# Two attention and feed-forward layers on one core: the second chunk's second weights and its last second products in another place of the order

## The chip, the core and the metric

The kernel runs on one core of a Trainium2 chip. Such a core has engines with instruction streams of their own: TensorE (PE) multiplies matrices, VectorE (DVE), ScalarE (ACT) and GpSimd (POOL) work on elements, SyncE (SP) mostly issues transfers. Each engine runs its own list strictly in order and waits on semaphores for the others. The metric is the device time of the whole program in microseconds (us).

## The reference, cut to what matters

One sequence of 2048 tokens with 576 numbers each goes twice through an attention layer and a feed-forward layer, with the same weights both times, all in fp32:

```
x = x + attention(layernorm(x), wqkv, wo)
x = x + silu(layernorm(x) @ w1) @ w2
x = x + attention(layernorm(x), wqkv, wo)
x = x + silu(layernorm(x) @ w1) @ w2
```

`w1` is 576 x 4608 and `w2` is 4608 x 576. The attention is sliding and dilated: 32 heads of 18 numbers, and token t sees only the tokens t, t-2, ..., t-14 (those that exist). Its logits and weighted sums are small products per token; the large matrix products are those of `wqkv`, `wo`, `w1` and `w2`.

## The kernel before, in words

**Chunks.** The tokens are cut into four chunks of 512 (four tiles of 128 tokens). With two layers that makes eight steps, numbered s = 0 to 7 in the code: attention, projection and feed-forward of the first, second, third, fourth chunk, and then the same again for the second layer. The front of a step (its attention on VectorE, the projection with `wo`, line L853, and the preparation of the feed-forward input) runs beside the feed-forward of the step before it. Where this document says "the second chunk" and "the third chunk" it means s = 1 and s = 2, in the first layer.

**Products.** Numbers that go through TensorE are split into a high and a low half in fp16; three matmuls (high by high, high by low, low by high) give one fp32 product.

**Two kinds of feed-forward.** Steps 0 and 1 use `ffn`. There the 4608 hidden numbers are 36 tiles of 128, taken in groups (of 9 for the second chunk, four groups). For each tile of a group there is a *first product* of 14 matmuls of 512 columns (L1192), written to one of two PSUM banks (z), then silu and scaling on ScalarE (L1194, L1196) and the low half on VectorE (L1199), which gives h. Then, for each of the four token tiles j, the *second products* (L1211) sum the nine h of the group into an accumulator (acc, two of them): three thirds of 18 matmuls of 288 columns. VectorE adds the accumulator to x (L860). Step 2 on use `ffn_pairs`: the first product is made in 2 x 2 blocks by a scheme with seven *block products* instead of eight (P5, P1, P3, P6, P2, P7, P4 in the order of `P_ORDER`), each 7 matmuls of 256 columns (L1095), with weights prepared once in DRAM (wfs). ScalarE copies some of the sums out (L1099), VectorE adds others (L1102), then come silu (L1118, L1120, L1122) and the two halves of h (L1125, L1128); second products (L1150) stand between the next block products.

**Forms.** Block products need seven sums and differences of the blocks of the layer-normalised input, called forms here. Each is made from two parts: ScalarE copies a high half (L1060, L1061) into a buffer yh or yo, VectorE subtracts for the low half (L1064, L1065), and SyncE transposes the part by a DMA (L1070) into the area xb. There are two buffers, used in turn, and each holds both parts of one form.

**Loads.** SyncE issues the weight loads: first weights of a tile (w1s, L865, 320 KB), second weights of a tile (w2s, L870, 288 KB), block weights (wfs, L1025, 160 KB each), and also the transposes of the projection's input (L465). GpSimd issues other transfers. First weights have 6 slots and block weights 12 in the same memory; second weights have 11 slots for all steps.

**What sets the order.** The code does not emit instructions at once. Each piece of work is an `op` with an engine, an estimated duration, what it reads and writes, and a priority (smaller goes first). A planner, `Plan.order`, simulates the engines, slots and transfers with these estimates, and on each engine takes the ready piece of the smallest priority whose slots are free. The instructions are then written in that order. In step s the products have priority pp = s + 0.5, and loads, ScalarE and VectorE work pd = s - 0.5. The block products of pair q have pp + 0.01 q, and their second products pp + 0.01 (...) + 0.005. The argument `after` adds an operation that the planner must have finished first; it moves an instruction in the lists, and no wait on the chip comes from it. `ffn_pairs` already uses it: `after=begun[-2:-1]` holds second weights of a pair back until an earlier pair has begun.

The functions that the diff touches, and what calls them:

Of the kernel before, what the change touches and what calls it, by code (L numbers as in the profile page):

```python
# [26 lines left out]
NJ = 4  # L27
# [5 lines left out]
NFT = F // P  # L33
# [231 lines left out]
def sliding_attention_silu_ffn(ctx: ExitStack, tc: tile.TileContext, x, wqkv, wo, w1, w2, out):  # L265
# [6 lines left out]
    op = S.op  # L272

    def fl(t):
        return t.rearrange("p a b -> p (a b)")
# [5 lines left out]
    def T(b):  # L281
        return S.tags[b.tag][b.slot]
# [154 lines left out]
    def passes(xk, wk):  # L437

        for k in range(4):
            yield xk(k), wk(k)  # L440
            yield xk(k), wk(5 + k)
            yield xk(5 + k), wk(k)
        yield xk(4), wk(4)
        yield xk(4), wk(9)
# [25 lines left out]
    PACE_WQ, PACE_WO, PACE_W = (1, 7, 0, 6), (2, 2, 3, 3, 3), (4, 5, 6, 7)  # L470
    gate = []
    formed = []
    begun = []
    highs = []
    turned = []
# [387 lines left out]
    def load_w1(f, prio):  # L863
        w = Buf("w1")
        op("SP", 0.38, lambda: nc.sync.dma_start(fl(T(w)), w1s[f]), [("w1s", f)], [w], prio, nbytes=P * 20 * P)  # L865
        return w

    def load_w2(f, prio, kind="w2", after=()):
        w = Buf(kind)
        op("SP", 0.38, lambda: nc.sync.dma_start(fl(T(w)), w2s[f]), [("w2s", f)], [w], prio, nbytes=P * 4 * D, after=after)  # L870
        return w
# [293 lines left out]
    def ffn(s, xT, xs):  # L1165
        raw = s == 0
        n, i = (G0, 0) if raw else (G1, 1)
        pp, pd = s + 0.5, s - 0.5
        for g in range(NFT // n):
            hb, wbs = [], []  # L1170
            if raw:
                ws = []
                for f in range(g * n, (g + 1) * n, NB):
                    for q in range(0 if f == 0 else NB, 2 * NB):
                        raw_load(f + q, -0.98 if f < NB else pd)
                    ws += raw_split(f, -0.98 if f < NB else pd)
                group_scale(0, g, g * n, (g + 1) * n)
            for f in range(g * n, (g + 1) * n):
                if raw:
                    wa, wb = ws[f - g * n]  # L1180
                    ka, kb = [(wa, 0), (wa, 1)], [(wb, 0), (wb, 1)]
                else:
                    wa, wb = load_w1(f, pd), load_w2(f, pd)
                    ka, kb = [wa], [wb]
                z, hs, h = Buf("z"), Buf("hs"), Buf("h")
                hb.append(h)
                wbs.append((wb, kb))

                def mm(z=z, wa=wa):
                    pl = list(passes(lambda k: T(xT)[:, k, :], lambda k: T(wa)[:, k, :]))  # L1190
                    for m, (u, v) in enumerate(pl):
                        nc.tensor.matmul(T(z), v, u, start=m == 0, stop=m == len(pl) - 1)  # L1192
                op("PE", 3.02, mm, [(xT, j) for j in range(NJ)] + ka, [z], pp)
                op("ACT", 0.61, lambda z=z, hs=hs, f=f: nc.scalar.activation(T(hs), T(z), AF.Silu, scale=d1[:, f:f + 1]),  # L1194
                   [z, ("s12", f)], [hs], pd, table="silu")
                op("ACT", 0.65, lambda hs=hs, h=h, f=f: nc.scalar.activation(T(h)[:, 0, :], T(hs), AF.Copy,  # L1196
                                                                             scale=shs[i][:, f:f + 1]),
                   [hs, ("sh", i, g)], [(h, 0)], pd)
                op("DVE", 0.68, lambda hs=hs, h=h, f=f: nc.vector.scalar_tensor_tensor(  # L1199
                    T(h)[:, 1, :], T(hs), shs[i][:, f:f + 1], T(h)[:, 0, :], op0=ALU.mult, op1=ALU.subtract),  # L1200
                   [hs, (h, 0), ("sh", i, g)], [(h, 1)], pd)
            for j in range(NJ):
                acc = Buf("acc")
                step = n if n < 6 else 3

                for t in range(0, n, step):
                    def mm2(j=j, acc=acc, t=t, step=step, hb=hb, wbs=wbs):
                        for q in range(t, t + step):
                            for m, (a, w) in enumerate(((0, 0), (0, 1), (1, 0))):
                                for h in range(2):  # L1210
                                    nc.tensor.matmul(T(acc)[:, h, 0:288], T(hb[q])[:, a, j * P:(j + 1) * P],  # L1211
                                                     T(wbs[q][0])[:, w, h * 288:(h + 1) * 288],
                                                     start=q == 0 and m == 0, stop=q == n - 1 and m == 2)
                    op("PE", 0.737 * step, mm2, [(hb[q], a) for q in range(t, t + step) for a in range(2)]
                       + [k for q in range(t, t + step) for k in wbs[q][1]], [acc], pp)
                op("DVE", 0.75, lambda j=j, acc=acc, g=g: add_to(xs[j], acc, d2s[i][:, g:g + 1]),
                   [acc, ("sh", i, g)], [xs[j]], pd)
        if raw:
            tables()
            pair_scale()  # L1220
        write_x(s, xs)
# [114 lines left out]
```

## Time and profile before

| | us |
|---|---|
| median of 3 runs | 2147.14 (2143.12 to 2147.98) |
| the profiled execution | 2146.88 |
| its span | 2144.9 |
| TensorE busy | 2115.3 (99% of the span) |
| VectorE busy | 1641.4 (77%) |
| ScalarE busy | 975.7 (45%) |
| GpSimd busy | 363.8 (17%) |

The granted TensorE clock is 0.999 of full speed over the whole execution. The second chunk's feed-forward ends at 684.66 us, and the third chunk's block products begin there.

How to read rows: in a group, `L1150 PE MATMUL acc<-w,h ... x5184 | 668.2, 286 | 1.5 <-DVE x L860 0.9` is line 1150 on TensorE, output and inputs by the program's names, the count, the busy time in us and the mean of one in ns, and behind the second bar the idle time of the engine just before these instructions with what ended most of it. In a timeline a row has its start and length in us, and the idle time before it in brackets. A row of transfers gives the queue, the count, the size of each and the median time from issue to landing in us. In a table of windows each engine has its busy time with the number of instructions in parentheses; then come the granted clock, the share of the DMA engines and GB/s.

### The profile page before, as it was taken

The page shows a single profiled execution, that of the slowest core. Times are in us where ns is not written, and L with a number is a line of the kernel's source. Part 1 is how long each engine was busy: PE and PEld are TensorE (multiplying, and loading weights), DVE is VectorE, ACT ScalarE, POOL GpSimd, SP SyncE. Part 2 cuts the span into 40 slices and gives each one's busy share as a digit, 9 for nine tenths or more (in the row PEclk, how much of TensorE's full clock was granted, in tenths as well). Part 3 has the DMA queues.
Part 4 walks back from the last instruction along what each step waited for, and adds up shares of the span by engine and source line. Part 5 has one row for each costly group of instructions (what it writes and reads, how often), then busy time and mean ns, then how long its engine had stood idle before and what let it go on. Part 6 is the DMA issues. An engine that isn't in the chain of part 4 may idle for free.

```text
span 2144.9 us, 41358 instructions
## 1 busy us (share of the span) xinstructions
PE 2115.3 (99%) x16233; PEld 1576.3 (73%) x16233; DVE 1641.4 (77%) x2599; ACT 975.7 (45%) x1803; POOL 363.8 (17%) x585
## 2 busy tenths in 40 slices
PE   9999999999999999999999999999999999999999
PEld 5556566656666788877788777887788877888887
DVE  8999999999877998558975499755997569853322
ACT  7555788644344554334433343343443434333332
POOL 2224656233232240001100010000000000000000
PEclk9999999999999999999999999999999999999999
DMA  6576777687888988676758755586555965566551
GB/s 182 158 224 249 251 267 249 189 280 238 191 210 256 298 255 248 153 224 169 220 133 194 218 173 174 139 246 182 168 166 147 254 180 161 163 156 198 155 168 62
DMA packets 334235, 426.21 MB, mean 199 GB/s; under 512 B 145608, under 2 KB 262708, under 8 KB 330072
## 3 DMA queue, kind: packets, MB, share of 16 engines
q1 hardware_dynamic: 293720, 293.19, 49.4%
q0 software_dynamic: 38304, 129.28, 19.2%
q8 instruction: 127, 2.08, 0.4%
q10 hardware_dynamic: 2016, 1.11, 0.2%
q14 instruction: 68, 0.56, 0.1%
HBM read 307.32 MB, written 67.68 MB: 175 GB/s over the span
## 4 chain that ended last, share of the span: by engine, by line
PE 76%; DVE 10%; DMA 8%; issue 5%; POOL 1%; ACT 1%; SPq 0%; DVEq 0%; ACTq 0%; POOLq 0%
PE acc L1150 26%; PE z L1095 12%; PE misc L1095 11%; PE z L681 8%; PE misc L681 5%; PE z L1192 5%; PE acc L853 4%; PE acc L1211 4%; DMA w<-wfs 2%; DMA wq<-in_B_w_dram 2%; DVE xa L1015 1%; DVE prs L814 1%; DMA xb<-yh 1%; DVE prs L821 1%; DVE prs L781 1%
## 5 line engine op out<-in xcount | busy, mean ns | idle before, releaser
L1150 PE MATMUL acc<-w,h 128*128 128x288 f16 x5184 | 668.2, 286 | 1.5 <-DVE x L860 0.9
L1150 PEld LDWEIGHTS <-h 128*128 128x128 f16 x5184 | 507.2, 98 | 126.5 <-issue 1.9
L1095 PEld LDWEIGHTS <-w 128*128 128x128 f16 x5292 | 517.1, 98 | 76.3 <-DMA w<-wfs 7.3
L1095 PE MATMUL z<-xb,w 128*128 128x256 f16 x2674 | 338.7, 273 | 6.0 <-DMA w<-wfs 4.7
L1095 PE MATMUL misc<-xb,w 128*128 128x256 f16 x2618 | 330.8, 273 | 1.5 <-ACT yo L1099 0.9
L860 DVE SCALAR_TENSOR_TENSOR x<-acc,d,x 128x576 f32<-128x576 f32 x183 | 148.4, 813 | 133.1 <-PE acc L1150 124.0
L1211 PE MATMUL acc<-w,h 128*128 128x288 f16 x1728 | 214.3, 286 | 0.0
L681 PEld LDWEIGHTS <-xa 128*128 128x128 f16 x1344 | 131.0, 98 | 113.3 <-issue 2.5
L1211 PEld LDWEIGHTS <-h 128*128 128x128 f16 x1728 | 168.4, 98 | 44.5
L814 DVE TENSOR_TENSOR prs<-kvs,pe 128x1152 f32<-128x1152 f32 x128 | 170.7, 1352 | 0.7
L781 DVE TENSOR_TENSOR prs<-qt,kvs 128x2304 f32<-128x2304 f32 x64 | 163.4, 2553 | 10.0 <-DMA kvs<-kvs 9.1
L785 DVE TENSOR_REDUCE lg<-prs 128x128 f32<-128x2304 f32 x64 | 163.1, 2548 | 1.0
L821 DVE TENSOR_TENSOR prs<-prs 128x1152 f32<-128x1152 f32 (+1 forms) x128 | 135.2, 1056 | 3.2
L1192 PE MATMUL z<-xb,w 128*128 128x512 f16 x588 | 130.5, 382 | 5.3 <-ACT hs L1194 1.8
L1128 DVE SCALAR_TENSOR_TENSOR h<-wq,sh,h 128x1024 f16<-128x1024 f32 x60 | 76.9, 1281 | 70.6 <-ACT h L1125 70.5
L681 PE MATMUL z<-wq,xa 128*128 128x432 f16 x630 | 120.4, 346 | 0.4 <-ACT w L694 0.4
L853 PE MATMUL acc<-wo,yo 128*128 128x288 f16 x896 | 114.4, 286 | 3.7 <-DMA yo<-yh 1.7
L1099 ACT ACTIVATE wq<-z 128x256 f32<-128x256 f32 x95 | 36.1, 380 | 174.3 <-PE z L1095 174.2
L1192 PEld LDWEIGHTS <-w 128*128 128x128 f16 x588 | 57.7, 99 | 75.5 <-issue 4.0
L681 PE MATMUL misc<-wq,xa 128*128 128x432 f16 x546 | 105.5, 346 | 2.6 <-ACT xa L463 1.3
L853 PEld LDWEIGHTS <-yo 128*128 128x128 f16 x896 | 87.3, 98 | 27.9 <-DMA yo<-yh 4.0
L762 POOL DMA_DIRECT2D kvs<-kvs x64 | 33.8, 535 | 419.7 <-ACT qt L750 419.7
(229 smaller groups left out, 2575.2 us busy)
## 6 DMA issues: line engine op xcount, KB each, us to landing
w<-wfs SPq DMA_DIRECT2D x756, 160.0 KB, 3.3
w<-w2s SPq DMA_DIRECT2D x252, 288.0 KB, 4.0
wq<-wqs SPq DMA_DIRECT2D x17, 1080.0 KB, 6.5
kvs<-kd POOLq DMA_DIRECT2D x8, 1584.0 KB, 9.7
w<-w1s SPq DMA_DIRECT2D x36, 320.0 KB, 5.8
wfs<-xa POOLq DMA_DIRECT2D x18, 640.0 KB, 5.4
w2s<-w POOLq DMA_DIRECT2D x36, 288.0 KB, 4.2
w1s<-wq POOLq DMA_DIRECT2D x30, 320.0 KB, 3.4
```

Of the source, the lines that this page charges most:

```text
L681: nc.tensor.matmul(T(m)[:, :3 * UC], a, b, start=n == 0, stop=n == len(pl) - 1)
L781: nc.vector.tensor_tensor(T(pr), T(qt)[:, j:j + 2, None, :].to_broadcast([P, 2, W, UC]), win(T(kv), j, 2), op=ALU.mult)
L785: nc.vector.tensor_reduce(T(lg)[:, j:j + 2].rearrange("p a w h -> p (a w h)"), T(pr).rearrange("p a w (h d) -> p (a w h) d", d=DH), axis=A ...
L814: nc.vector.tensor_tensor(T(pr)[:, a].rearrange("p w (h d) -> p w h d", d=DH), v, T(pe)[:, j + a, :, :, None].to_broadcast([P, W, UH, DH]) ...
L821: nc.vector.tensor_tensor(t[:, :, 0:h, :], t[:, :, 0:h, :], t[:, :, h:2 * h, :], op=ALU.add)
L853: nc.tensor.matmul(T(acc)[:, h, 0:288], a, b[:, h * 288:(h + 1) * 288], start=n == 0, stop=n == len(pl) - 1)
L860: nc.vector.scalar_tensor_tensor(t, T(acc)[:, :, 0:288], d, t, op0=ALU.mult, op1=ALU.add)
L1095: nc.tensor.matmul(t, w[:, u, :], v[:, r, :], start=first and m == 0, stop=m == 6, skip_group_check=True)
L1128: op("DVE", 1.2, lambda hq=hq, h=h, sc=sc: nc.vector.scalar_tensor_tensor(T(h)[:, 1].rearrange("p f t -> p (f t)"), T(hq).rearrange("p r t ...
L1150: nc.tensor.matmul(T(acc)[:, h, 0:288], T(hb[t])[:, a, f, j * P:(j + 1) * P], T(wbs[t][f])[:, w, h * 288:(h + 1) * 288], start=t == 0 and ...
L1192: nc.tensor.matmul(T(z), v, u, start=m == 0, stop=m == len(pl) - 1)
L1211: nc.tensor.matmul(T(acc)[:, h, 0:288], T(hb[q])[:, a, j * P:(j + 1) * P], T(wbs[q][0])[:, w, h * 288:(h + 1) * 288], start=q == 0 and m = ...
```

## The change

Three edits, of which the last two belong together:

- `load_w2` in the second chunk's feed-forward gets an `after`: from the third tile of a group on, the load of a tile's second weights is ordered after an earlier first product (`hidden[-2:][:1]`, the last but one that was listed when this load is listed). The first two tiles of each group have none.
- The list `hidden` collects the first products for that.
- The second products of the second chunk's last group (`g + 1 == NFT // n`) get the priority pp + 1 + 0.01 j + 0.004 in place of pp. With s = 1 that is 2.504, 2.514, 2.524 and 2.534 for the four token tiles: the third chunk's block products of pairs 0 to 3 have 2.50, 2.51, 2.52 and 2.53, so the planner puts each token tile behind the ready block products of one pair.

The first chunk's feed-forward (raw) and all steps from the third chunk on keep their code.

```diff
@@ -470,6 +470,7 @@
     formed = []
+    hidden = []
     begun = []
@@ -1180,7 +1181,7 @@
                 else:
-                    wa, wb = load_w1(f, pd), load_w2(f, pd)
+                    wa, wb = load_w1(f, pd), load_w2(f, pd, after=hidden[-2:][:1] if f % n > 1 else ())
                     ka, kb = [wa], [wb]
@@ -1190,7 +1191,7 @@
-                op("PE", 3.02, mm, [(xT, j) for j in range(NJ)] + ka, [z], pp)
+                hidden.append(op("PE", 3.02, mm, [(xT, j) for j in range(NJ)] + ka, [z], pp))
@@ -1212,7 +1213,8 @@
                     op("PE", 0.737 * step, mm2, [(hb[q], a) for q in range(t, t + step) for a in range(2)]
-                       + [k for q in range(t, t + step) for k in wbs[q][1]], [acc], pp)
+                       + [k for q in range(t, t + step) for k in wbs[q][1]], [acc],
+                       pp if raw or g + 1 < NFT // n else pp + 1 + 0.01 * (j + 0) + 0.004)
```

The changed kernel is one line longer from L473 on and two from L1217 on; L1095 of before is L1096 there. Three places show what the planner makes of it.

**TensorE, from the last first product of the second chunk on** (z and misc are PSUM banks, w_70 the area of first and block weights, w_93 that of second weights, xb the transposed input). Before; 54 matmuls for each token tile, and the block products after all four:

```order
L1192 MATMUL z_101<-xb,w_70 128x512
L1211 MATMUL acc_105<-w_93,h 128x288
L1211 MATMUL acc_104<-w_93,h 128x288
...
L1095 MATMUL z_100<-xb,w_70 128x256
L1095 MATMUL z_101<-xb,w_70 128x256
```

And of the change, with 7 matmuls for each row of L1096 and 18 for each row of L1212:

```order
L1193 MATMUL z_101<-xb,w_70 128x512
L1096 MATMUL z_100<-xb,w_70 128x256
L1096 MATMUL misc_102<-xb,w_70 128x256
L1212 MATMUL acc_104<-w_93,h 128x288
L1096 MATMUL z_100<-xb,w_70 128x256
L1096 MATMUL misc_102<-xb,w_70 128x256
L1212 MATMUL acc_104<-w_93,h 128x288
L1096 MATMUL z_101<-xb,w_70 128x256
L1212 MATMUL acc_104<-w_93,h 128x288
```

The 216 second matmuls of the last group, which stood in one piece between the last first product and the first block product, now stand in thirds of a token tile between block products; the first two block products come directly behind the last first product.

**SyncE, at the transposes of the third chunk's first four forms and the loads behind them** (the transposes of the second, third and fourth form before; of all four in the change). Before:

```order
L1070 DMA_TRANSPOSE xb<-yo 128x5x128 x2
L1070 DMA_TRANSPOSE xb<-yh 128x5x128 x2
L870 DMA w_93<-w2s_189 128x1152
L870 DMA w_93<-w2s_190 128x1152
L870 DMA w_93<-w2s_191 128x1152
L1070 DMA_TRANSPOSE xb<-yo 128x5x128
L870 DMA w_93<-w2s_192 128x1152
L870 DMA w_93<-w2s_193 128x1152
L870 DMA w_93<-w2s_194 128x1152
L1070 DMA_TRANSPOSE xb<-yo 128x5x128
```

And of the change:

```order
L1071 DMA_TRANSPOSE xb<-yh 128x5x128 x2
L1071 DMA_TRANSPOSE xb<-yo 128x5x128 x2
L1071 DMA_TRANSPOSE xb<-yh 128x5x128 x2
L1071 DMA_TRANSPOSE xb<-yo 128x5x128 x2
L871 DMA w_93<-w2s_189 128x1152
L866 DMA w_70<-w1s_157 128x1280
L871 DMA w_93<-w2s_190 128x1152
L866 DMA w_70<-w1s_158 128x1280
L871 DMA w_93<-w2s_191 128x1152
```

The last group's second weights stood between the transposes; now the transposes stand in one piece ahead of them, and second and first weights alternate.

**ScalarE, at the copies for the forms and the evacuation of first products.** Before:

```order
L1060 ACTIVATE yh<-prs 128x288
L1061 ACTIVATE yh<-prs 128x32
L1194 ACTIVATE hs<-z_101,d_264 128x512
L1196 ACTIVATE h<-hs,sh_266 128x512
L1194 ACTIVATE hs<-z_100,d_264 128x512
L1196 ACTIVATE h<-hs,sh_266 128x512
L1194 ACTIVATE hs<-z_101,d_264 128x512
L1196 ACTIVATE h<-hs,sh_266 128x512
L1060 ACTIVATE yo<-o 128x288
L1061 ACTIVATE yo<-o 128x32
```

And of the change:

```order
L1061 ACTIVATE yh<-prs 128x288
L1062 ACTIVATE yh<-prs 128x32
L1061 ACTIVATE yo<-o 128x288
L1062 ACTIVATE yo<-o 128x32
L1061 ACTIVATE yo<-prs 128x288
L1062 ACTIVATE yo<-prs 128x32
L1195 ACTIVATE hs<-z_101,d_264 128x512
L1197 ACTIVATE h<-hs,sh_266 128x512
```

The copies of the buffer yo (those of the sixth form), which followed three evacuations in the order before, now stand ahead of the first of them.

## What the change does to the time: the prediction

> **What bounds the kernel now.** First the page's head and its busy row, then the table of windows over the stretch that the change touches (columns: TensorE busy, its weight loads, VectorE, ScalarE, GpSimd, granted clock, DMA share, GB/s), with one late window beside it.
>
> ```profile
> span 2144.9 us, 41358 instructions
> PE 2115.3 (99%) x16233; PEld 1576.3 (73%) x16233; DVE 1641.4 (77%) x2599; ACT 975.7 (45%) x1803; POOL 363.8 (17%) x585
> ...
> 550.00:600.00 50.00, 47.57 (x300) 28.85 (x298) 41.14 (x72) 17.77 (x24) 14.80 (x22) 1.00 0.96 234
> 600.00:650.00 50.00, 48.18 (x317) 30.90 (x316) 35.15 (x70) 24.74 (x51) 20.63 (x30) 1.00 0.95 230
> 650.00:700.00 50.00, 45.90 (x354) 34.38 (x353) 40.39 (x51) 19.09 (x34) 14.52 (x24) 1.00 0.88 258
> 700.00:750.00 50.00, 48.52 (x421) 40.62 (x419) 47.08 (x57) 27.10 (x44) 11.53 (x17) 1.00 0.92 291
> ...
> 1600.00:1650.00 50.00, 50.00 (x427) 41.61 (x426) 38.04 (x77) 14.97 (x30) 0.00 (x0) 1.00 0.55 141
> ```
>
> TensorE bounds the whole kernel: 99% of the span, and full in a late window. Time is to be had only from its gaps, and these four windows hold 2.43 + 1.82 + 4.10 + 1.48 = 9.83 us of them, a third of the 29.6 us idle in the whole span. The change adds and removes no arithmetic, so 9.83 us is the most that it can win here. TensorE's timeline says where the gaps lie (start, length, line, tiles, count, and in brackets the idle time before with what ended it).
>
> ```profile
> 563.45 3.60 PE L853 MATMUL acc<-wo,yo 128*128 128x288 f16 x28 [1.16 <-DMA yo<-yh]
> 576.86 3.60 PE L853 MATMUL acc<-wo,yo 128*128 128x288 f16 x28 [0.75 <-DVE mx L794]
> 587.04 3.60 PE L853 MATMUL acc<-wo,yo 128*128 128x288 f16 x28 [0.53 <-DMA yo<-yh]
> ...
> 637.05 21.31 PE L1192 MATMUL z<-xb,w 128*128 128x512 f16 x98 [1.82 <-ACT hs L1194]
> 658.20 2.00 PE L1211 MATMUL acc<-w,h 128*128 128x288 f16 x15
> ...
> 684.66 3.22 PE L1095 MATMUL z<-xb,w 128*128 128x256 f16 x28
> 687.72 0.93 PE L1095 MATMUL misc<-xb,w 128*128 128x256 f16 x7
> ...
> 690.64 0.92 PE L1095 MATMUL misc<-xb,w 128*128 128x256 f16 x7 [0.47 <-ACT yo L1099]
> ...
> 694.25 0.92 PE L1095 MATMUL misc<-xb,w 128*128 128x256 f16 x7 [0.39 <-ACT yo L1099]
> 698.42 0.94 PE L1095 MATMUL z<-xb,w 128*128 128x256 f16 x7 [3.24 <-DMA w<-wfs]
> ...
> 705.08 0.94 PE L1095 MATMUL z<-xb,w 128*128 128x256 f16 x7 [1.20 <-DMA w<-wfs]
> ...
> 715.53 0.94 PE L1095 MATMUL misc<-xb,w 128*128 128x256 f16 x7 [0.27 <-DMA w<-wfs]
> ```
>
> Three places: the third chunk's projection (1.16 + 0.75 + 0.53 = 2.44 us), one wait of 1.82 us for ScalarE at 637, and the start of the third chunk's block products (0.47 + 0.39 + 3.24 + 1.20 + 0.27 = 5.57 us). From 684.66 on, block products run alone: 28 matmuls in 687.72 - 684.66 = 3.06 us, so a product of 7 takes 0.77 us and a pair of blocks 5.4 us. The second chunk's last second products stand before them, from 658.20 to 684.66: 26.5 us, 6.6 us for each of four token tiles.
>
> **Why the gap is there.** SyncE's queue and the transfers of 684 to 706:
>
> ```profile
> 685.98 0.91 SPq L870 DMA_DIRECT2D w<-w2s  x2
> 690.87 20.37 SPq L1025 DMA_DIRECT2D w<-wfs  x15
> ...
> w<-wfs SPq DMA_DIRECT2D x14, 160.0 KB, 11.2
> w<-w2s SPq DMA_DIRECT2D x5, 288.0 KB, 3.8
> ```
>
> A pair of blocks eats 7 x 160 + 2 x 288 KB = 1.70 MB; in 5.4 us that is 314 GB/s, against the 291 GB/s that all queues together moved in the window from 700. When the last second product ends, nine slots of second weights come free at once, SyncE sends their loads between the block weights, and a block weight then needs 11.2 us to land.
>
> **The change part by part.** (1) *The second products among the block products.* The order of the changed kernel puts 20 block products and all 216 second matmuls into one stretch before the first second product of the third chunk: 20 x 0.77 + 26.5 = 41.9 us for 20 x 160 KB, 76 GB/s. Its second weights need slots that these second products still hold, so they can no longer crowd in at the start. The three DMA gaps lose their cause; the two waits for ScalarE's copies (0.86 us) get 2.2 us of second products between most products of one bank. What is late next, with the end of the last first product (658.20 here) as zero:
>
> The seven forms of the input: the fifth (P2) is due after four block products and two thirds of a tile, 4 x 0.77 + 4.4 = 7.5 us; the sixth at 10.4; the seventh (P4) at 17.2.
>
> ```profile
> 656.13 2.57 SPq L1070 DMA_TRANSPOSE xb<-yh  x2
> ...
> 660.57 0.44 ACT L1060 ACTIVATE yh<-o 128x288 f16<-128x288 f32 x1 [0.73 <-DMA xb<-yh]
> ...
> 666.37 2.57 SPq L1070 DMA_TRANSPOSE xb<-yh  x2
> ```
>
> P2's transposes stay behind the same ten block-weight loads, so I keep 656.13; a buffer is free, that is landed, at 660.57, 4.4 us after. That is 2.4 on my scale, 5 us ahead of need. P4's left at 666.37, 8.2 on the scale; its second one leaves 1.3 us later and with 4.4 us is down at 13.9, 3.3 us ahead. So no wait if transposes land as here. The first h of the third chunk needs a slot that the last tile's first third frees; 36 second matmuls and two block products follow, 5.9 us, against 1.15 + 1.28 us for its two steps:
>
> ```profile
> L1128 DVE SCALAR_TENSOR_TENSOR h<-wq,sh,h 128x1024 f16<-128x1024 f32 x60 | 76.9, 1281 | 70.6 <-ACT h L1125 70.5
> L1125 ACT ACTIVATE h<-wq,sh 128x1024 f16<-128x1024 f32 x60 | 68.9, 1148 | 1.9
> L860 DVE SCALAR_TENSOR_TENSOR x<-acc,d,x 128x576 f32<-128x576 f32 x183 | 148.4, 813 | 133.1 <-PE acc L1150 124.0
> L785 DVE TENSOR_REDUCE lg<-prs 128x128 f32<-128x2304 f32 x64 | 163.1, 2548 | 1.0
> ```
>
> The adds of the four tiles (L860, 0.81 us) use two accumulators and have over 6 us each. VectorE is 47.08 us of 50 busy from 700 on, and a reduce of 2.55 us ahead of a small add can hold a bank once or twice. Bounds for what stays of the 5.57: 0, and 5.9 (rival A). I take 1.4, about half such a reduce, since every cover named is longer than the step under it: 4.2 us won.
>
> (2) *The second weights held back.* This moves loads only; the `after` puts no wait on the chip, it shifts them in SyncE's list. Loads of 288 KB land in 3.8 us (5.5 at 612 to 637, below), and the moved ones still stand three first products (3 x 3.03 = 9 us) ahead of their use: 9 us over 5.5, cost nothing; without that cover one would cost up to 5.5 us. What was queued behind them is freed:
>
> ```profile
> 625.57 1.59 SPq L870 DMA_DIRECT2D w<-w2s  x3
> 627.26 4.73 SPq L1070 DMA_TRANSPOSE xb<-yo  x1
> 632.08 1.48 SPq L870 DMA_DIRECT2D w<-w2s  x3
> ...
> 631.98 0.44 ACT L1060 ACTIVATE yo<-prs 128x288 f16<-128x288 f32 x1 [5.69 <-DMA xb<-yo]
> ...
> 636.34 0.67 ACT L1194 ACTIVATE hs<-z,d 128x512 f32<-128x512 f32 x1
> ...
> 642.07 0.43 ACT L1060 ACTIVATE yo<-prs 128x288 f16<-128x288 f32 x1
> ...
> w<-w2s SPq DMA_DIRECT2D x9, 288.0 KB, 5.5
> xb<-yo SPq DMA_TRANSPOSE x4, 12.2
> ```
>
> The 1.82 us at 637 is the evacuation of a first product (L1194, 636.34) behind a copy for a form that sat 5.69 us on a transpose. Now the price: in the new order the copies for six forms all stand before that evacuation, the sixth too, which here ran at 642.07, 5.7 us after it. So the chain of forms must come earlier. It does by the projection: its four tiles stand after one first product of the next group, the first two back to back; from 532.2 (the start of the tile group before it) 26.5 + 3 x 3.03 + 4 x 3.43 = 49.3 puts its end at 581.5, against 587.04 + 3.43 = 590.5. Nine us earlier, of which VectorE's new order (3.4 us of the preparation moved ahead of the statistics) eats about 2. The sixth copy then ends near 635.5; it has to end near 631, one first product after the evacuated one, less the 5 us that it was ready before 642 (its transposes left by 634.9). I leave 1.2 of the 1.82, bounds 0 and 7.8 (rival B): 0.6 won. In the projection the transposes no longer wait behind six loads of second weights, but tiles three and four follow closer; half of 2.44 us, 1.2 won, bounds 0 and 4.
>
> Sum: 4.2 + 0.6 + 1.2 = 6.0 us. The profiled execution took 2146.88 us (span 2144.9 and 2.0 around it), so 2140.9; its time stands 0.26 us under the median of the runs shown, 2147.14. Forecast 2141.
>
> **The rivals.** *A. New waits take the place of the old at the block start.* Transposes of the window 612 to 637 needed 12.2 us to land, not 4.4. With that P2's second part, which leaves 1.3 us after 656.13, lands at 11.4 on my scale, 3.9 us after it is due; P7, due at 10.4 + 3.9 = 14.3, is down at 14.1; P4, due at 21.1, lands at 21.7. That is 3.9 + 0.6 = 4.5 us, with VectorE's 1.4 some 5.9, and the 5.57 come back. For it: the DMA share of 0.95 to 0.96 up to 650. Against: the 0.73 us row at 660.57. Time 2146.9 - 1.8 + 0.3 = 2145.4.
>
> The Trainium skill, "DMA: Bandwidth & Descriptors", section "Issuing engines are not separate DMA queues", says that transfers of all queues run on the same 16 engines and interleave. By it, held-back weights would meet these transposes whatever queue they use; the 11.2 us row agrees that loads slow each other.
>
> *B. The form copies hold ScalarE (the other side).* If the chain of forms gains nothing, the sixth copy ends at 642.5 while the third first product of that group needs its bank at 635: with the evacuation of 0.67 us behind it 7.8 us of waiting in place of 1.82, so +6.0; the late forms leave 2.5 of the block gaps, -3.1. 2146.9 + 6.0 - 3.1 = 2149.8. It decides from a chain that comes less than 3 us earlier. For it: the whole chain is paced by transposes at a DMA share of 0.95. Against: the projection's place.
>
> The Trainium skill, "TensorE: Matmul & The Clock Gate", section "HAM oscillation — how this bites in real kernels", warns of idle gaps over some 3.4 us, after which the clock is halved. By it a gap of 7.8 us would cost an estimated 1.7 us more (3.4 us at half speed), 2151.5. The longest gap here, 3.24 us, shows a clock of 1.00 in its window, so no run here shows it.
>
> *C. The gain stops at the fourth chunk's projection,* which waits for VectorE's attention:
>
> ```profile
> 838.84 2.02 SPq L465 DMA_TRANSPOSE yo<-yh  x1
> ...
> 848.06 3.59 PE L853 MATMUL acc<-wo,yo 128*128 128x288 f16 x28
> ```
>
> From the end of the issue (840.9) 7.2 us pass; 4.4 are needed to land, so 2.8 of 6.0 us are covered and 3.2 would return: 2144.1. Against it: SyncE sends this transpose between block weights whose slots TensorE frees, so it moves along.
>
> **How the numbers follow.** Forecast 0.50 (own range 2137.0, all 9.83 us gone, to 2143), A 0.22, B 0.17, C 0.11. The likeliest is 2141. Eight in ten: 2137 to 2149, to just short of B. Below 0.2% of the time (4.3 us, what a measurement of this kernel can tell from no change) counts as same: faster means under 2142.8. Forecast gives 0.47 faster and 0.03 same; A 0.04 and 0.18; C 0.01, 0.08 and 0.02 slower; B 0.03 same, 0.14 slower. Together 0.52, 0.32, 0.16.
>
> **What would show it.** Right: in the changed trace no idle over 1 us with block weights as releaser among the first 20 block products; their landing well under 11.2 us; the copies for the sixth form done before about 631; TensorE full after. Wrong: an evacuation of L1192's bank by L1194 that waits several us (B), transposes as releasers of the first block products (A), or idle at the fourth chunk's projection (C). A gap that none of these names would break the sum itself.

## The result and the profile after

The changed kernel takes 2141.9 us in the median of 15 runs (2139.36 to 2145.52), the kernel before 2147.14 us (2143.12 to 2156.66, 15 runs). The ratio is 0.997, with a 95% interval of 0.9961 to 0.998: 0.3% faster, 4 to 8 us. The forecast was 2141 us, with 2137 to 2149 as its range. The profiled execution took 2141.49 us, its span is 2139.6 us against 2144.9.

First the page's head and its busy row, then the table of windows over the same stretch as before the change (TensorE busy, weight loads, VectorE, ScalarE, GpSimd, granted clock, DMA share, GB/s).

```profile
span 2139.6 us, 41351 instructions
PE 2114.5 (99%) x16233; PEld 1576.2 (74%) x16233; DVE 1640.1 (77%) x2599; ACT 977.0 (46%) x1803; POOL 365.9 (17%) x585
...
550.00:600.00 50.00, 48.02 (x308) 29.79 (x306) 47.20 (x83) 21.38 (x29) 19.74 (x28) 1.00 0.85 222
600.00:650.00 50.00, 50.00 (x327) 31.82 (x325) 34.71 (x72) 23.38 (x49) 21.30 (x30) 1.00 0.99 243
650.00:700.00 50.00, 50.00 (x400) 38.96 (x398) 42.40 (x52) 22.07 (x39) 10.68 (x17) 1.00 0.99 281
700.00:750.00 50.00, 49.71 (x431) 41.81 (x429) 47.40 (x61) 28.22 (x45) 21.01 (x31) 1.00 1.04 323
```

TensorE's idle time in the four windows is 1.98 + 0 + 0 + 0.29 = 2.27 us, where it was 9.83. All of the gain, and more, is in this stretch: 7.6 us against a span that is 5.3 us shorter. The rest lies outside: 12.97 us of idle in the first 300 us became 14.71, although TensorE's order is the same there in both kernels, from 750 to the end of the span 6.8 us became 8.1, and TensorE was busy 0.7 us less. TensorE's timeline shows which waits are left (start, length, line, tiles, count, and in brackets the idle time before with what ended it).

```profile
567.31 3.60 PE L854 MATMUL acc<-wo,yo 128*128 128x288 f16 x28 [0.41 <-DMA yo<-yh]
575.50 3.60 PE L854 MATMUL acc<-wo,yo 128*128 128x288 f16 x28 [1.56 <-DMA yo<-yh]
...
629.98 27.36 PE L1193 MATMUL z<-xb,w 128*128 128x512 f16 x126
657.18 0.93 PE L1096 MATMUL z<-xb,w 128*128 128x256 f16 x7
...
664.64 0.93 PE L1096 MATMUL z<-xb,w 128*128 128x256 f16 x7
...
683.40 6.78 PE L1212 MATMUL acc<-w,h 128*128 128x288 f16 x54
690.01 0.93 PE L1096 MATMUL z<-xb,w 128*128 128x256 f16 x7
690.78 6.78 PE L1212 MATMUL acc<-w,h 128*128 128x288 f16 x54
...
715.83 0.94 PE L1096 MATMUL z<-xb,w 128*128 128x256 f16 x7 [0.29 <-DMA w<-wfs]
...
906.31 0.93 PE L1096 MATMUL misc<-xb,w 128*128 128x256 f16 x7 [0.86 <-DVE hs L1103]
907.67 0.92 PE L1096 MATMUL z<-xb,w 128*128 128x256 f16 x7 [0.43 <-ACT wq L1100]
```

The nine first products of the last group run through without the gap of 1.82 us (629.98, 126 matmuls), and the block start has lost all five of its gaps; 0.29 us is all that waits for a block weight. The projection still waits 0.41 + 1.56 us for its transposes, about as much as before. The rows at 906 and 908 are new in size: the start of the fourth chunk's block products waits 1.29 us for VectorE and ScalarE, where before had 0.45 us at 914.

The block products now begin at 657.18, among the second products. SyncE's list from there on, and the landing of the block weights sent from 657 to 684:

```profile
661.34 2.91 SPq L1026 DMA_DIRECT2D w<-wfs  x6
666.96 7.11 SPq L1026 DMA_DIRECT2D w<-wfs  x7
675.36 15.93 SPq L1026 DMA_DIRECT2D w<-wfs  x7
691.71 1.79 SPq L871 DMA_DIRECT2D w<-w2s  x3
...
w<-wfs SPq DMA_DIRECT2D x19, 160.0 KB, 2.6
```

Up to 691 no second weight stands among the block weights, and these land in 2.6 us. The crowd of second weights has not gone, it comes later. The transfers of 684 to 706:

```profile
w<-w2s SPq DMA_DIRECT2D x9, 288.0 KB, 8.3
w<-wfs SPq DMA_DIRECT2D x4, 160.0 KB, 12.8
```

Nine second weights go out here, nearly in one piece (five in these 22 us before the change), and the block weights of that time need 12.8 us to land, more than the 11.2 us of before. They delay nobody: from 683.40 to 697.4 TensorE works on the last two token tiles, with one block product between them. So a crowd alone does not make a gap, and the experiments ask what else it takes.

### The profile page after: what moved, and what is told of

The parts are those of the page before. It is cut to its first block, busy times and chain, and to the rows that moved or that the text cites. A ratio compares the mean times of both kernels' runs of the same rounds, so it can differ in the third digit from the quotient of the medians.

```text
span 2139.6 us, 41351 instructions
## 1 busy us (share of the span) xinstructions
PE 2114.5 (99%) x16233; PEld 1576.2 (74%) x16233; DVE 1640.1 (77%) x2599; ACT 977.0 (46%) x1803; POOL 365.9 (17%) x585
## 4 chain that ended last, share of the span: by engine, by line
PE 88%; DMA 6%; DVE 3%; issue 1%; ACT 1%; SPq 1%; POOL 0%; ACTq 0%; DVEq 0%; POOLq 0%
PE acc L1151 28%; PE z L1096 13%; PE misc L1096 13%; PE z L1193 9%; PE acc L1212 9%; PE z L682 7%; PE acc L854 5%; PE misc L682 5%; DMA w<-wfs 1%; DMA xb<-yo 1%; DMA h<-in_A_wqkv_dram 1%; DMA w<-in_B_w_dram 1%; DMA w<-w2s 1%; DMA yo<-yh 0%; DMA x<-xd 0%
## 5 line engine op out<-in xcount | busy, mean ns | idle before, releaser
L1096 PEld LDWEIGHTS <-w 128*128 128x128 f16 x5292 | 517.3, 98 | 72.0 <-DMA w<-wfs 3.7
L1096 PE MATMUL z<-xb,w 128*128 128x256 f16 x2653 | 335.5, 273 | 2.3 <-DMA w<-wfs 1.7
L1096 PE MATMUL misc<-xb,w 128*128 128x256 f16 x2639 | 335.7, 273 | 1.1 <-DVE hs L1103 0.9
L1212 PE MATMUL acc<-w,h 128*128 128x288 f16 x1728 | 215.4, 286 | 0.0
L1212 PEld LDWEIGHTS <-h 128*128 128x128 f16 x1728 | 168.4, 98 | 44.2
L682 PE MATMUL misc<-wq,xa 128*128 128x432 f16 x518 | 99.1, 346 | 2.7 <-ACT xa L463 1.3
## 6 DMA issues: line engine op xcount, KB each, us to landing
w<-w2s SPq DMA_DIRECT2D x252, 288.0 KB, 4.4
w2s<-w POOLq DMA_DIRECT2D x36, 288.0 KB, 4.1
```

Source lines behind the costliest of these rows:

```text
L682: nc.tensor.matmul(T(m)[:, :3 * UC], a, b, start=n == 0, stop=n == len(pl) - 1)
L1096: nc.tensor.matmul(t, w[:, u, :], v[:, r, :], start=first and m == 0, stop=m == 6, skip_group_check=True)
```

## The experiments

Each was timed beside the kernel before. Line numbers are those of the changed kernel. Single profiles of one instruction list differ: the first 300 us alone had 13.0 to 15.7 us of idle in all profiles of this study. So one profile tells which wait is there, and the timing what it is worth. Three of the profiles below are of executions 3.5 to 4.6 us under the median of their kernel: the first of the products alone (2139.0 us), that of the second weights alone (2145.32 us) and that of the loads held back (2142.67 us).

### The two parts apart

Only the products moved:

```diff
-                    wa, wb = load_w1(f, pd), load_w2(f, pd, after=hidden[-2:][:1] if f % n > 1 else ())
+                    wa, wb = load_w1(f, pd), load_w2(f, pd)
```

> Only the priority of the last group's second products is changed; the second weights are ordered as before. Theory (two separate gains): the block start's five gaps, 5.57 us, fall to under 1.5 as in the changed kernel (0.29), while the gap of 1.82 us at 637 and the projection's 2.44 us stay, so TensorE's idle between 550 and 750 is some 4.3 to 5.5 us and the time some 4 to 5 us under the kernel before, 0.998. Rival (the products need the front that the held-back weights bring): the fifth to seventh form are late for the early block products, transposes release them with 3 us and more, and the time is within 1 us of before.

Only the second weights held back:

```diff
-                       pp if raw or g + 1 < NFT // n else pp + 1 + 0.01 * (j + 0) + 0.004)
+                       pp)
```

> Only the second weights are held back; the last second products stand in one piece as before. Theory: the projection moves earlier and the form copies stand ahead of the evacuations, the gap at 637 goes (under 0.5) and the projection's idle is near 2.0, but the block start keeps its gaps of 5 to 6 us with block weights as releaser: idle between 550 and 750 of 7 to 8 us, the time 2 to 2.5 us under before, 0.999. Rival (one lump of second weights is what crowds the block weights, wherever the products stand): the block start's gaps fall under 2 us too, and the time is 5 us under before.

And the changed kernel once more:

> The changed kernel once more. Theory: idle of TensorE between 550 and 750 again near 2.3 us, and the gaps outside it that its first profile has and before has not (2.57 us at 262, 1.44 us at 1281) are of one execution: at least one of them is smaller by 1 us or gone here. Rival (the change pays back 1.4 us in the fifth chunk): the gap at 1281 with block weights as releaser is there again. Ratio to before 0.9965 to 0.998.

| | median, us | ratio to before, interval |
|---|---|---|
| products alone | 2143.59 | 0.998 (0.9967 to 0.9994) |
| second weights alone | 2149.41 | 0.9998 (0.9986 to 1.001) |
| both, again | 2141.34 | 0.9967 (0.9953 to 0.9981) |

The products alone bring most of the gain, the second weights alone nothing that can be measured. TensorE's gaps with the products alone, in a first profile and then in a second one of the same kernel:

```profile
564.81 3.60 PE L854 MATMUL acc<-wo,yo 128*128 128x288 f16 x28 [0.93 <-DMA yo<-yh]
665.00 0.93 PE L1096 MATMUL z<-xb,w 128*128 128x256 f16 x7 [1.41 <-DMA xb<-yh]
```

```profile
564.41 3.60 PE L854 MATMUL acc<-wo,yo 128*128 128x288 f16 x28 [0.90 <-DMA yo<-yh]
635.66 21.31 PE L1193 MATMUL z<-xb,w 128*128 128x512 f16 x98 [1.09 <-ACT hs L1195]
667.10 1.09 PE L1096 MATMUL z<-xb,w 128*128 128x256 f16 x7 [2.66 <-DMA xb<-yh]
```

Neither expectation fits whole. No block weight is late (theory), but the fifth form's transposes are, by 1.41 and 2.66 us (rival). The gap at 637 is absent in the one and 1.09 us in the other, though ScalarE's list there is that of before: it is a matter of chance between 0 and 1.8 us.

Why the fifth form is late can be read from the queues. Its transposes leave SyncE at 653.89 in the first profile, not later but earlier than the 656.03 of the changed kernel. In that time GpSimd fetches weights that are prepared for later steps. Its queue q0 over 653 to 667 (packets, MB, share of the DMA engines), with the products alone and then in the changed kernel:

```profile
q0 software_dynamic: 596, 1.29, 49.4%
```

```profile
q0 software_dynamic: 6, 0.02, 0.4%
```

The second profile of the products alone has 1.50 MB there, the other two of the changed kernel 0.04 MB or less. So with the products alone the transposes meet GpSimd's transfers; in the changed kernel those went out before. This is read from the traces; no run tests it by itself.

With the second weights alone the rows are:

```profile
567.37 3.60 PE L854 MATMUL acc<-wo,yo 128*128 128x288 f16 x28 [1.04 <-DMA yo<-yh]
577.09 3.60 PE L854 MATMUL acc<-wo,yo 128*128 128x288 f16 x28 [3.09 <-DMA yo<-yh]
697.20 0.93 PE L1096 MATMUL misc<-xb,w 128*128 128x256 f16 x7 [1.69 <-DVE yo L1103]
700.46 1.67 PE L1096 MATMUL z<-xb,w 128*128 128x256 f16 x7 [2.34 <-DMA w<-wfs]
```

The gap at 637 is gone, the projection pays for it with 4.13 us, and the block start keeps 4.02 of 5.57 us. The places are those of the theory; its gain of 2 us did not come. The median, 4 us above the profiled execution, has losses that this profile does not show.

The repetition of the changed kernel shows 1.44 us at 1281 to be of one execution (it is absent). The wait near 907 is there again: 1.3 to 1.7 us between 900 and 921 in all three profiles of the changed kernel, 0.71 us in the one of before. That one belongs to the change, and to its two parts together: neither the products alone (two profiles) nor the second weights alone wait there.

A second comparison of the products alone and the changed kernel:

> The second products among the block products alone, once more. If the held-back weights are worth nothing beside it, its time is within 1 us of the changed kernel's of this call, and their profiles' idle between 550 and 750 is 2 to 3 us in both. If they are worth the 2 us of the gap at 637, the gap at 637 is there in this profile (1 to 2 us), and the changed kernel is 2 us or more ahead. In either case a wait of 1 to 1.5 us for the fifth form's transposes near 665 is expected again.

> The changed kernel, for comparison with the run of the products alone in the same call. Projection idle 2 to 3 us, no gap at 637, block start under 0.5 us; ratio to before 0.9965 to 0.998.

The products alone took 2142.5 us, 0.9979 (0.9966 to 0.9992), the changed kernel 2141.95 us, 0.9973 (0.9962 to 0.9984). The profile of the products alone has the gap at 637 with 1.09 us, and the fifth form 2.66 us late. The times differ by 0.6 us in the medians and 1.9 us in the means (2143.57 and 2141.72); in the first comparison it was 2.2 us in both. The profiles do not say where this comes from. Over 550 to 750 the products alone waited 2.45 and 4.79 us, the changed kernel 2.27, 2.93 and 2.80; from 750 to the end it was 6.4 and 4.7 us against 8.1, 7.5 and 9.0, so what the held-back weights remove in the one stretch is lost again, and more, in the other. Whether they add something to the products is not settled.

### Is it the crowd of second weights?

The prediction held that second weights push the block weights aside. In the kernel before, with TensorE's order left nearly alone (one piece of second products, then 16 block products in place of 15), the loads were held back instead:

```diff
-                w2b = [load_w2(2 * q + f, pd, after=begun[-2:-1] if q > q0 + 1 else ()) for f in range(2)]
+                w2b = [load_w2(2 * q + f, pd, after=ended[-1:] if s == S2 and q < 6 else begun[-2:-1] if q > q0 + 1 else ()) for f in range(2)]
...
-                product("P4", a, False, True)
+                ended.append(product("P4", a, False, True))
```

> The kernel before, with the second weights of the third chunk's first six pairs each ordered after the last block product of the pair before; TensorE's order stays one piece of second products, then 16 block products. Theory (second weights crowd the block weights out): the gaps of 3.24 and 1.20 us with block weights as releaser go, those of 0.47 and 0.39 us with ScalarE's copies stay, the block weights land in under 6 us in place of 11.2; 4 us under before, 0.998. Rival (the block weights are late by what lies on the engines anyway, or by the slots): the two gaps stay or move a few products on, and the time is within 1 us of before.

2146.18 us, ratio 0.9986 (0.9971 to 1.0001). Transfers of 684 to 706, and TensorE's gaps:

```profile
w<-wfs SPq DMA_DIRECT2D x16, 160.0 KB, 7.1
...
690.52 0.93 PE L1096 MATMUL misc<-xb,w 128*128 128x256 f16 x7 [0.47 <-ACT yo L1100]
696.03 0.94 PE L1096 MATMUL z<-xb,w 128*128 128x256 f16 x7 [2.29 <-DMA w<-wfs]
698.52 1.65 PE L1096 MATMUL misc<-xb,w 128*128 128x256 f16 x7 [0.47 <-DMA x<-in_A_x_dram]
716.71 0.94 PE L1096 MATMUL misc<-xb,w 128*128 128x256 f16 x7 [0.41 <-DMA w<-wfs]
```

The landing fell from 11.2 to 7.1 us, but the block start still loses 3.64 of 5.57 us. By this one profile the crowd is about a third of it, 1.9 us, and the interval of the time just includes no gain. What SyncE waited for in 684 to 706 shows the rest, before (first) and here:

```profile
SPq L1025 <- DMA w<-wfs: 8.3, 3, 4.5
SPq L1025 <- PE z L1095: 5.7, 2, 5.5
```

```profile
SPq L1026 <- PE z L1096: 12.2, 6, 10.0
SPq L871 <- DMA w<-wfs: 4.8, 2, 3.1
```

By the profile, SyncE before stood 8.3 us on earlier block weights that had not landed, and could not issue the next. In both kernels it stood in one long wait on a block product, 5.5 and 10.0 us, that is on a slot: the twelve slots are full until the first block product runs, and nothing can be fetched ahead. A load that goes out when the first of twelve products ends is due eleven products later, 11 x 0.77 = 8.5 us; with 7 to 11 us to land it has little or nothing to spare.

### Is it the time between the block products?

If so, the second products must stand spread among the block products. One priority for all four tiles leaves 7 block products ahead of the last second product in place of 18, and a double step sets the tiles farther apart at first:

```diff
-                       pp if raw or g + 1 < NFT // n else pp + 1 + 0.01 * (j + 0) + 0.004)
+                       pp if raw or g + 1 < NFT // n else pp + 1 + 0.004)
```

> The changed kernel with one priority for all four token tiles of the last group, so that 7 block products stand among them in place of 20 and nine thirds follow nearly in one piece. Theory (what helps is time for the block weights: 12 slots hold 9 us of block products run alone): the first 13 or so products after the last third run alone again, together with the second weights' loads, and a gap of 1 to 3 us with block weights as releaser comes back behind them; idle at 650 to 750 of 1.5 to 3.5 us, 0.998. Rival (it is enough that the first block products and the second weights' slots come apart): idle there under 0.5 us as in the changed kernel.

```diff
-                       pp if raw or g + 1 < NFT // n else pp + 1 + 0.01 * (j + 0) + 0.004)
+                       pp if raw or g + 1 < NFT // n else pp + 1 + 0.02 * (j + 0) + 0.004)
```

> The changed kernel with twice the step between the priorities of the four token tiles (0.02 for 0.01): the thirds stand farther apart at first and the last six in one piece. Theory (time for the block weights is what counts, and the changed kernel has no block weight late any more): block products wait for no block weight before the last six thirds, gaps under 1 us up to 700; but two pairs of block products follow the last piece nearly alone, and 0 to 2 us of waiting comes back behind it; within 2 us of the changed kernel. Rival (the farther apart, the better, and the changed kernel's step still costs time somewhere): 1 us or more under the changed kernel.

The lump took 2150.46 us, 1.0011 (0.9999 to 1.0023): all of the gain is gone, and 5.93 us of idle stand between 690 and 750. The wide step took 2142.08 us, 0.9967 (0.9952 to 0.9982), as the changed kernel, without an idle row between 690 and 750. The lump's gaps behind the last second product, and SyncE's longest wait over 690 to 750:

```profile
704.23 1.70 PE L1096 MATMUL z<-xb,w 128*128 128x256 f16 x14 [0.71 <-DMA w<-wfs]
707.88 0.94 PE L1096 MATMUL misc<-xb,w 128*128 128x256 f16 x7 [1.19 <-DMA w<-wfs]
747.50 1.68 PE L1096 MATMUL misc<-xb,w 128*128 128x256 f16 x7 [4.03 <-DMA w<-wfs]
...
SPq L1026 <- DMA w<-w2s: 14.4, 12, 2.1
```

The 1.90 us come where the theory put them. The 4.03 us at 747 it did not foresee: the second weights of the next pairs come in one piece again, and SyncE waits 14.4 us, in twelve waits, for second weights to land before it issues the next block weight. So the spread is needed, and twice the spread brings no more. The lump does not tell time and crowd apart, since it has too little of the one and too much of the other; the loads held back above and the changed kernel's 684 to 706 do.

### What do the held-back weights do?

They were kept in the last group alone, and in the other three groups alone:

```diff
-                    wa, wb = load_w1(f, pd), load_w2(f, pd, after=hidden[-2:][:1] if f % n > 1 else ())
+                    wa, wb = load_w1(f, pd), load_w2(f, pd, after=hidden[-2:][:1] if f % n > 1 and g + 1 == NFT // n else ())
```

> The changed kernel, with the second weights held back in the second chunk's last group alone; the projection keeps the place of the kernel before, the transposes of the forms have no second weights between them. Theory (holding back in the groups before moves the projection and only trades one wait for another: 2 to 4 us in the projection for 1.8 us at 637): projection idle near 1 to 2.4 us, no gap over 0.5 us at 630 to 640, block start under 1.5 us; idle between 550 and 750 of 2 to 3.5 us and a time within 1.5 us of the changed kernel, 0.9965 to 0.998. Rival (the form copies need the earlier projection): the copies of the sixth form now stand ahead of the first evacuation of the last group with the old projection, and a gap of 4 to 8 us opens at 635; the time is that of before or above.

```diff
-                    wa, wb = load_w1(f, pd), load_w2(f, pd, after=hidden[-2:][:1] if f % n > 1 else ())
+                    wa, wb = load_w1(f, pd), load_w2(f, pd, after=hidden[-2:][:1] if f % n > 1 and g + 1 < NFT // n else ())
```

> The changed kernel, with the second weights held back in the second chunk's first three groups and not in the last; the last group's nine loads stand in one piece behind the transposes of the first four forms. Theory (the earlier projection, which the groups before bring, is what lets the form copies stand ahead of the evacuations): projection idle 2 to 4 us as in the changed kernel, no gap over 0.5 us at 630 to 640, block start under 1 us; within 1.5 us of the changed kernel. Rival (the last group's alternation of loads is what counts): the nine second weights in one piece delay the first weights or the block weights behind them, with a gap of 1 to 3 us at 636 to 660, or the fifth form's transposes late near 665 as where only the products were moved.

In the last group alone: 2147.17 us, 0.9994 (0.9982 to 1.0005). In the others alone: 2141.58 us, 0.9963 (0.9948 to 0.9979). The first expectation failed on both sides, since neither 4 to 8 us opened at 635 nor was it as fast as the changed kernel. Its rows:

```profile
639.68 21.31 PE L1193 MATMUL z<-xb,w 128*128 128x512 f16 x98 [1.77 <-ACT hs L1195]
683.29 1.65 PE L1096 MATMUL misc<-xb,w 128*128 128x256 f16 x7 [2.10 <-DMA xb<-yh]
```

The gap at 637 stays, and the seventh form is late; another 4.6 us of idle lie between 750 and 1300, where before had 2.2. In the others alone neither is there, but the projection waits 4.69 us. So what counts are the held-back weights of the groups before the last. They bring the earlier projection, and with it another list on ScalarE: in the last group alone 3.08 us of weight preparation (L1009, at 634.17) still stand just ahead of the evacuation that the gap waits for, in the others alone they do not. The last group's weights can be left as they were.

### A version that beats both

The waits left are those of the projection: its third tile is listed before its transpose has landed. The planner was told that the third chunk's projection transposes move 1.6 times their bytes, which moves nothing else but the order:

```diff
-                  nbytes=P * 9 * P * 4)
+                  nbytes=P * 9 * P * 4 * late)
...
-            transposed(oh, lambda oT=oT: T(oT), oT, j, pr_, s < 2)
+            transposed(oh, lambda oT=oT: T(oT), oT, j, pr_, s < 2, 1.6 if s == S2 else 1)
```

> The changed kernel, with the third chunk's projection transposes counted 1.6 times as large by the planner alone, so that the four tiles of the projection stand two after two first products and two after two more, one first product later than in the changed kernel; the block products keep their order. Theory (in the changed kernel the third tile is listed before its transpose has landed, 1.6 to 2.0 us, and the first is short by 0.4 to 0.9): the projection's idle falls from 2 to 2.8 us to under 1 us, the forms come no later by more than 0.5 us, nothing opens at 637; 1 to 2 us under the changed kernel, 0.996 to 0.9975. Rival (what the projection waits for is VectorE's chain, and whoever gives it time there pays at the form copies): the gap at 637 comes back with 1 to 3 us and the time is that of the changed kernel or above.

> The version with the later projection once more, since its lead rests on few runs. Theory: ratio to before of 0.9935 to 0.9965, and in the profile one wait of 1 to 2 us in the projection (the third tile), nothing at 637 and no block weight late. Rival (the lead was chance): 0.9965 to 0.998, as the changed kernel.

2138.1 us, 0.9946 (0.9926 to 0.9966), and again 2138.62 us, 0.9954 (0.9938 to 0.997). That is 3 to 4 us under the changed kernel's medians (2141.34 to 2141.95). The two were not timed side by side; timed beside the first of these runs were the wide step and the others alone, 2142.08 and 2141.58 us. The second run's only gap in the stretch:

```profile
579.36 7.03 PE L854 MATMUL acc<-wo,yo 128*128 128x288 f16 x56 [1.38 <-DMA yo<-yh]
```

The projection waits 1.4 to 1.75 us in place of 2.0 to 2.75 (under 1 was expected), and nothing came back at 637. This explains about 1 us. The profiles of the two versions also differ by 1 to 2 us in TensorE's busy time (2112.5 and 2113.5 against 2114.3 to 2114.9 us) for the same arithmetic; why is left open.

## Why the prediction was right, and where not

The time was right to 1 us, in part by luck: the errors of its terms go both ways. Beside each predicted gain stands what the profiles show. The changed list has three profiles; the old list of the projection and of the form copies has four (before, the products alone twice, and the loads held back in the kernel before).

| step | predicted gain | measured |
|---|---|---|
| block start (5.57) | 4.2 | 5.3 to 5.5: 0.29, 0.18, 0.08 left |
| gap at 637 | 0.6 | 0 left; the old list had 1.82, 0, 1.09, 1.18, so 1.0 on average |
| projection | 1.2 | 1.97, 2.75, 2.72 against 2.44, 0.93, 0.90, 2.74: 0.7 lost on average |
| fourth chunk's start | 0 | 0.6 to 1.0 lost at 907 |

The measured terms add up to some 5.4 + 1.0 - 0.7 - 0.8 = 4.9 us, the predicted ones to 6.0; the medians lie 5.2 us apart.

**Block start.** The main term was right, and too small by a little over 1 us: the 1.4 us kept for VectorE holding a bank did not appear. The forms came as worked out. The fifth was due 7.5 us after the last first product: the row at 664.64 starts 7.46 us after 657.18, without a wait.

**Its reason** held for the new order and was too narrow for the old one. The prediction said that second weights "can no longer crowd in at the start" and asked for a landing well under 11.2 us. At the new block start none is sent, and the landing is 2.6 us. For the old gap, though, it named the second weights alone. Holding them back in the old order removed only 1.9 us, where 4 were expected. What is left fits another cause, time: block products run alone behind twelve full slots. The prediction had the figure for that too, 76 GB/s once the products are spread in place of 314, and the one edit removes both causes. (Its two rates count a KB as 1000 bytes. The profile counts 1024, as a second weight of 128 x 1152 two-byte numbers has 288.0 KB; the rates are 78 and 322 GB/s, and nothing changes by it.)

**The gap at 637.** The place was right, the cause was half of it, and the deadline was wrong. The prediction laid the gap to a copy that sat on a transpose until 631.98. Between that copy and the evacuation at 636.34, ScalarE did 3.9 us of work that waited for nothing: two more copies and, in front of them, a piece of weight preparation:

```profile
632.45 3.08 ACT L1008 ACTIVATE xa<-wq,accw 128x1024 f16<-128x1024 f32 x4
```

The same 3.08 us stand there in every profile that has this gap, and in the first of the products alone, where the copy came at 629.24 and TensorE did not wait. In the changed kernel none stands between copy and evacuation, it follows from 636.07 on, so a copy that is 2.3 us later than before does no harm.

The prediction wanted the sixth form's copies done by 631. ScalarE's timeline of the changed kernel:

```profile
634.27 0.44 ACT L1061 ACTIVATE yo<-prs 128x288 f16<-128x288 f32 x1 [2.50 <-DMA xb<-yo]
634.62 0.21 ACT L1062 ACTIVATE yo<-prs 128x32 f16<-128x32 f32 x1
634.74 0.67 ACT L1195 ACTIVATE hs<-z,d 128x512 f32<-128x512 f32 x1
```

They end at 634.8, and the evacuation behind them at 635.4. The third first product needs that bank at 629.98 + 2 x 3.03 = 636.0. Rival B's own sentence had this bank needed at 635; the sum's 631 took one first product too much off. The margin is 0.6 us (1.4 and 1.7 in the other two profiles), so B was nearer than the timing shows. That the copies ended 0.7 us ahead of the 635.5 of the sum is luck: its projection was to end at 581.5, 9 us earlier than before, and ended at 585.4, 5 us earlier.

**The projection.** Nothing was won. That the transposes are no longer queued behind six loads was said; that the third and fourth tile follow closer, weighed at half, took more than that back.

**The rivals.** A was right as a mechanism, and in another kernel: with the products alone the fifth form's transposes release a block product 1.41 and 2.66 us late. In the changed kernel GpSimd's transfers are out of their way, which joins the two parts that the prediction summed apart. C did not occur: the fourth chunk's projection shows no gap. What was given back lies later, at the start of its block products. B's long wait did not occur; what it said of the clock is taken up at the end.

## What to carry to other kernels

Where a stage change starts a consumer that eats its loads faster than they land, its buffers are full but stand still until it starts: the slots, less the one in use, times the time of one step must exceed the landing time. Work of the old stage that needs no new loads, spread among the first steps, gives that time; put among them in one lump, with the second weights close behind it, it gave nothing. An edit to a planner's priorities or loads also moves work on engines that it does not name, so look for the engine whose order it changed (here the projection, and the weight preparation on ScalarE and GpSimd) before crediting the edit.

## What was not expected of the hardware

Short gaps cost more than their length, and not always. The granted clock in steps of 5 us, after a gap of 2.10 us (second weights held back in the last group alone) and after one of 2.66 us (products alone, second profile):

```profile
683.00:688.00 5.00, 4.71 (x27) 3.28 (x27) 1.88 (x4) 0.87 (x2) 0.00 (x0) 0.66 0.51 149
```

```profile
665.00:670.00 5.00, 2.90 (x16) 2.08 (x17) 1.78 (x4) 3.02 (x6) 0.00 (x0) 0.77 1.14 264
670.00:675.00 5.00, 5.00 (x40) 4.00 (x39) 3.45 (x5) 1.56 (x4) 0.67 (x2) 0.89 0.76 200
```

The clock is 0.66, and 0.77 then 0.89. Before the change, behind its gap of 3.24 us, it stayed at 1.00:

```profile
694.00:699.00 5.00, 1.50 (x13) 1.11 (x13) 4.82 (x7) 3.35 (x6) 2.29 (x4) 1.00 1.00 389
```

The Trainium skill, "TensorE: Matmul & The Clock Gate", section "HAM oscillation — how this bites in real kernels", warns of idle gaps over some 3.4 us. Here gaps of 2.1 and 2.7 us were enough, and one of 3.2 us was not, so the length alone did not decide. Other profiles say the same: the clock fell behind gaps of 2.04 and 4.03 us (the lump) and stayed at 1.00 behind one of 3.09 us (second weights alone).

In the two executions above, 1.7 us of clock are lost on top of the gap, as much as the prediction estimated for B (0.34 x 5 us in the one, 0.23 x 5 + 0.11 x 5 us in the other). The 18 second matmuls that come next show it: they took 3.16 and 3.75 us, where the changed kernel's first 18 took 2.20. A sum made of idle time alone, as in the prediction, misses this.
